# Order of VectorE and ScalarE in a turn of an attention kernel with two MLPs behind it

## The chip, the cores and the metric

One core of a Trainium2 chip. The metric is device time in microseconds of one execution, the median of the runs. TensorE multiplies, VectorE and ScalarE work element by element on SBUF and PSUM, GpSimd on SBUF alone, SyncE issues DMAs. Each engine executes its own instructions strictly in program order and waits for the others by semaphores.

## The reference

```
proj = x @ w_phi;  proj -= max(|proj|) over the features
phi(x) = [exp(proj), exp(-proj)]
kv = phi(k)^T v;  z = sum of phi(k) over the sequence
attn = (phi(q) kv) / (phi(q) z + 1e-6)
y = leaky(attn_rows @ w_in1, 0.01) @ w_out1
h = y @ w_in2;  out = (h * tanh(softplus(h))) @ w_out2
```

q, k, v are (4, 8, 576, 64) in fp32, w_phi is (64, 128), and the MLPs work on 2304 rows of 512 with 2048 hidden features. The weights of the MLPs arrive as 64-bit floats; the kernel turns them into fp32 itself.

## The kernel before

**Pairs and turns.** The 32 heads are worked on as 16 pairs. `attention(n)` (L513), called for n = 0 to 16, is one turn of a software pipeline over five pairs at once: t = n+2 has its q and k transposed, p = n+1 is projected, w = n gets its exponentials and its kv product, o = n-1 its numerator and denominator, x = n-2 is transposed into X, the input of the first MLP. Products of fp32 are made of three matmuls of split operands (`three`, L83, lines 84 to 86).

**What a turn does, in program order.** Loads for pair n+3 and values for t are issued on SyncE. `conv0.begin` is VectorE's part of the weight conversion: clamp of the high words to `c` (L135), a shift of the low words inside the stage (L137), and the mask and or to `e` (L138). `q_proj` (L389) makes four matmul groups; ScalarE copies each out of PSUM into `qd` (L401), and behind each second copy GpSimd computes the absolute maximum over the partitions, `qm` (L406, two per turn). `x_left` (L468) scales the left-over columns of x on ScalarE into `xleft`. `conv0.scale` (L143) makes on ScalarE the high part `wh` of the last converted weight (L213) and scales the newest `c` (L150). `k_proj` (L367) makes two groups, three in odd turns; VectorE takes their maximum `mx` and subtracts it (`kd`, L363 and L364). `k_exp` takes both exponentials of w on ScalarE (`kp`, in even turns `lp` as well, L386). `x_t` (L475) transposes `xn` on TensorE into `xt`, ScalarE copies it to X (L481), a matmul with `fold` puts the left-over columns into the last 64 columns of the PSUM tile `outs`, and a small ScalarE copy takes them to X (L484). `transposes` (L328) turns q and k of t, `split` on ScalarE and VectorE makes the high and low parts, and `q_left` adds two small casts (L359). `nd` (L434) writes numerator and denominator into `outs`, of which there is one: it must wait until every reader of the last contents is done, the small copy L484 among them. `normalise` (L454) reads them on VectorE (`den`, a reciprocal, `xn`). `q_guard` (L408) subtracts `qm` from `qd`, with both operands in SBUF. `conv0.join` puts sign and scaled value together on VectorE (L157) and makes the low part `wl` of the last weight (L214), or sends the converted weight to DRAM. Then come the exponentials of q, both halves of `kv` (L412) and a ScalarE copy of it (L432).

**Buffers that couple the engines.** The PSUM ring "a" has four banks. The q and k projections and the transposes of t take them in program order, so the transposes of k wait until the first k group has been read (L364), and k_proj until the q copies (L401) are done. `outs`, `kvp` and `xt` exist once. The stage has two buffers: the load of the next but one unit waits for the last reader of its buffer, and SyncE's later DMAs stand behind it in the queue.

**Conversion.** `conv0` has 15 units, one per turn from turn 1 on. The first ten are split into `wh` and `wl` one turn after their join, the last five are stored to DRAM.

**Around it.** Behind turns 8 to 11 `window(0, ...)` splits a quarter of the first block of X (ScalarE, then VectorE). Turns 15 and 16 end with `moe(0)` and `moe(1)`, the first hidden products of the first MLP: TensorE, then ScalarE, VectorE, ScalarE, VectorE (`leaky`). Behind turn 16 the last pair gets its `x_left` and `x_t`, and the loop of `moe` takes over.

Of the kernel before, what the change touches and what calls it, by code (L numbers as in the profile page):

```python
# [10 lines left out]
F32 = mybir.dt.float32  # L11
F32R = mybir.dt.float32r
AF = mybir.ActivationFunctionType
ALU = mybir.AluOpType
# [9 lines left out]
def attention_two_mlps_kernel(  # L24
# [12 lines left out]
    nc = tc.nc  # L37
    B, H, S, D = q.shape
    NT, DM = out.shape
    DFF = w1_in.shape[1]  # L40
    F = w_phi.shape[1]
    P = 128
    KD = DM // P
    M = DFF // P
    MAIN = 512
# [5 lines left out]
    CONV0 = 1  # L51
    HEAD = 2
    PAIRS = B * NP
# [6 lines left out]
    I32 = mybir.dt.int32  # L60
# [3 lines left out]
    gp = tc.alloc_tile_pool(name="gp", bufs=2)  # L64
# [3 lines left out]
    dr = tc.alloc_tile_pool(name="dr", bufs=1, space=bass.MemoryType.DRAM)  # L68
    ap = tc.alloc_tile_pool(name="ap", bufs=2, reuse_waits="tile")

    X = xp.tile([P, KD, NT], F32, name="X")
# [7 lines left out]
    def split(hi, lo, src):  # L79
        nc.scalar.activation(out=hi, in_=src, func=AF.Copy)  # L80
        nc.vector.tensor_tensor(out=lo, in0=src, in1=hi.bitcast(F32), op=ALU.subtract)
# [11 lines left out]
    class Conv:  # L93
# [4 lines left out]

        def __init__(self, which, units):
            self.which, self.units, self.at, self.loaded = which, units, 0, 0  # L100
            self.stage, self.open, self.half, self.rest = {}, None, None, None

        def load(self, ahead):

# [19 lines left out]
        def begin(self):  # L124

            self.load(1)
            if self.at == len(self.units):
                return
            u, kind = self.units[self.at]
            self.at += 1  # L130
            c = gp.tile([P, DM], F32, tag="c", name="c")
            e = gp.tile([P, DM], I32, tag="w1", name="e", bufs=1)
            stg = self.stage.pop(u)
            hw, lw = stg[:, :, 1], stg[:, :, 0]
            nc.vector.tensor_scalar(out=c, in0=hw.bitcast(F32), scalar1=F64_TOP, scalar2=-F64_TOP,  # L135
                                    op0=ALU.min, op1=ALU.max)
            nc.vector.tensor_scalar(out=lw, in0=lw, scalar1=29, scalar2=None, op0=ALU.logical_shift_right)  # L137
            nc.vector.scalar_tensor_tensor(out=e, in0=hw, scalar=-(1 << 31), in1=lw,  # L138
                                           op0=ALU.bitwise_and, op1=ALU.bitwise_or)
            self.load(1)  # L140
            self.open = (u, kind, c, e)

        def scale(self):  # L143

            if self.half is not None:
                u, c = self.half
                self.half, self.rest = None, split_w(self.which, u // 2, u % 2, c)
            if self.open is not None:
                c = self.open[2]
                nc.scalar.activation(out=c, in_=c, func=AF.Copy, scale=2.0 ** -112)  # L150

        def join(self):

            if self.open is not None:
                u, kind, c, e = self.open
                self.open = None
                nc.vector.scalar_tensor_tensor(out=c.bitcast(I32), in0=c.bitcast(I32), scalar=3, in1=e,  # L157
                                               op0=ALU.logical_shift_left, op1=ALU.bitwise_or)
                if kind == "store":
                    scr[self.which, u] = dr.tile([P, DM], F32, name=f"scr{self.which}_{u}")  # L160
                    nc.sync.dma_start(out=scr[self.which, u], in_=c)
                else:
                    self.half = (u, c)
            if self.rest is not None:
                self.rest()
                self.rest = None

        def step(self, *between):
            between = list(between) + [lambda: None] * 2
# [37 lines left out]
    def split_w(which, m, x, src):  # L207

        if x == 0:
            pool = wp0 if m < EARLY else wp  # L210
            W[which, m] = [pool.tile([P, 2, KD, P], F32R, tag=f"{t}{m}", name=f"w{t}{m}") for t in "hl"]
        hi, lo = (t[:, x].rearrange("p k f -> p (k f)") for t in W[which, m])
        nc.scalar.activation(out=hi, in_=src, func=AF.Copy)  # L213
        return lambda: nc.vector.tensor_tensor(out=lo, in0=src, in1=hi.bitcast(F32), op=ALU.subtract)  # L214
# [34 lines left out]
    with tc.manual_schedule():  # L249
# [105 lines left out]
        def q_left(i):  # L355
            s, l = st[i], lf[i // 2]
            c = P + (i % 2) * LEFT
            for x in "hl":
                nc.vector.tensor_copy(out=s["q" + x][:, HM:HM + LEFT], in_=l[x][:, c:c + LEFT].bitcast(F32))  # L359
# [69 lines left out]
        def kv_copy(i):  # L429
            s = st[i]  # L430
            s["kv"] = ap.tile([P, 4, D + 1], F32, tag="kv", name="kv", bufs=1)
            nc.scalar.activation(out=s["kv"], in_=s["kvp"][:, 0:4 * (D + 1)].rearrange("p (c n) -> p c n", n=D + 1), func=AF.Copy)  # L432
# [21 lines left out]
        def normalise(i):  # L454
            s = st[i]
            N = D + 1
            t = s["nd"]
            den = s["den"] = ap.tile([P, 2, 5], F32, tag="den", name="den")
            nc.vector.tensor_scalar(out=den, in0=t[:, :, D:5 * N:N], scalar1=1e-6, scalar2=None, op0=ALU.add)
            nc.vector.reciprocal(out=den, in_=den)  # L460
            s["xn"] = ap.tile([P, NM, 2, D], F32, tag="xn", name="xn")
            nc.vector.tensor_tensor(
                out=s["xn"].rearrange("p (c u) h d -> p c (u h) d", c=2),
                in0=t[:, :, 0:4 * N].rearrange("p c (m n) -> p c m n", n=N)[:, :, :, 0:D],
                in1=den[:, :, 0:4].unsqueeze(3).to_broadcast([P, 2, 4, D]), op=ALU.mult)
            s["xl"] = xleft[i % 2]

        def x_left(i):  # L468

            s = st[i]  # L470
            for h, r in enumerate(HALVES):
                nc.scalar.activation(out=s["xl"][r, h], in_=s["nd"][r, 1, 4 * (D + 1):4 * (D + 1) + D], func=AF.Copy,  # L472
                                     scale=s["den"][r, 1, 4:5])

        def x_t(i):  # L475
            s = st[i]
            b, p = divmod(i, NP)
            t = pa.tile([P, 512], F32, tag="xt", name="xt")
            for j in range(NM):
                nc.tensor.transpose(out=t[:, j * P:(j + 1) * P], in_=s["xn"][:, j].rearrange("p h d -> p (h d)"), identity=ident)  # L480
            nc.scalar.activation(out=X[:, p, b * MAIN:(b + 1) * MAIN], in_=t, func=AF.Copy)  # L481
            o = s["nd"][:, 1, MAIN - LEFT:MAIN]
            nc.tensor.matmul(out=o, lhsT=s["xl"].rearrange("p h d -> p (h d)"), rhs=fold, start=True, stop=True)
            nc.scalar.activation(out=X[:, p, C0 + b * LEFT:C0 + (b + 1) * LEFT], in_=o, func=AF.Copy)  # L484
            st[i] = None

        def k_exp(i, a):
            sg = 1 - 2 * a
            if i % 2 == 0:
                lf[i // 2].setdefault("lp", []).append(exp(lf[i // 2]["kd"], "lp", sg))  # L490
            st[i].setdefault("kp", []).append(exp(st[i]["kd"], "kp", sg))
# [21 lines left out]
        def attention(n):  # L513

            x, o, w, p, t = (i if 0 <= i < PAIRS else None for i in range(n - 2, n + 3))
            if n + 3 < PAIRS:
                load(n + 3)
            if t is not None and t > 1:  # L520
                values(t)
            if n >= CONV0:
                conv0.begin()
            if p is not None:
                for c in range(4):
                    q_proj(p, c)
            if x is not None:
                x_left(x)
            if n >= CONV0:
                conv0.scale()  # L530
            if p is not None:
                for c in range(2):
                    k_proj(p, c)
                if p % 2 == 0:
                    k_proj_left(p)
            if w is not None:
                for a in range(2):
                    k_exp(w, a)
            if x is not None:
                x_t(x)  # L540
            if t is not None:
                transposes(t)
                q_left(t)
            if o is not None:
                nd(o)
                normalise(o)
            if p is not None:
                q_guard(p)
            if n >= CONV0:
                conv0.join()  # L550
            if w is not None:
                st[w]["qp"] = [exp(st[w]["qd"], "qp", sg) for sg in (1, -1)]
                for a in range(2):
                    kv(w, a)
                kv_copy(w)
            if p is None:
                moe(n - PAIRS + 1)

# [212 lines left out]
        for n in range(PAIRS + 1):  # L771
            attention(n)
            if 0 <= n - PAIRS // 2 < KD:
                window(0, (n - PAIRS // 2,))
        x_left(PAIRS - 1)
        x_t(PAIRS - 1)
        ap.release()
        pa.release()
        rings["b"] = tc.alloc_tile_pool(name="pb", bufs=4, space=PSUM)
# [43 lines left out]
```

## Time and profile before

| | us |
|---|---|
| median of 3 runs (1012.76 to 1013.44) | 1013.23 |
| the profiled execution | 1010.47 |
| its span | 1008.6 |
| TensorE busy (PE) | 965.0 |
| VectorE busy (DVE) | 729.6 |
| ScalarE busy (ACT) | 510.6 |
| GpSimd busy (POOL) | 73.5 |
| stage loads: 64 of 512 KB, issue to landing | 3.7 and 3.6 |

Mean granted TensorE clock: 0.984 of full speed. The profile is one execution; the busy time of an engine counts from an instruction's start to its end, and neighbours may overlap by about 0.1 us, so that the sum of an engine can come close to a stretch that is full. A releaser is the event that the profile takes to have ended an engine's idle time; PEld is TensorE's weight load, which runs beside its matmuls. A wait on "issue" has no releaser that the profile shows.

### The profile page before, as it was taken

What the parts mean: (1) busy time and instruction counts of PE and PEld (TensorE: products, weight loads), DVE (VectorE), ACT (ScalarE), POOL (GpSimd) and SP (SyncE); (2) the same over time, 40 slices, a digit from 0 to 9 for tenths busy, and PEclk for the clock granted to TensorE, in tenths of its full rate; (3) what the DMA queues carried; (4) which work ended last, traced back from release to release, by engine and by line L of the source; (5) the groups of instructions that cost most, each with busy time, mean ns of one, the idle gap of its engine ahead of it and who ended that gap; (6) DMA issues with size and microseconds to landing.
All of it is one profiled execution on the core that took longest, in us unless ns stands there. A gap on an engine that the chain in (4) does not pass through costs nothing.

```text
span 1008.6 us, 16736 instructions
## 1 busy us (share of the span) xinstructions
PE 965.0 (96%) x6704; PEld 827.9 (82%) x6704; DVE 729.6 (72%) x1271; ACT 510.6 (51%) x886; POOL 73.5 (7%) x36
## 2 busy tenths in 40 slices
PE   8888878789999999999999999999999999999998
PEld 7788778668888889988888888888888988888886
DVE  7998998528984666666434457978877888878976
ACT  5887777635553333343234445545544555445543
POOL 3533333100000000000000000000000000000000
PEclk9999998889999999999999999999999999999999
DMA  6544423114431444444301330000100100001001
GB/s 199 142 134 119 113 79 111 36 64 139 153 105 53 143 148 133 142 144 147 115 0 45 121 96 11 1 1 1 42 1 1 43 1 22 0 1 42 1 1 42
DMA packets 68205, 72.97 MB, mean 72 GB/s; under 512 B 27168, under 2 KB 52640, under 8 KB 68128
## 3 DMA queue, kind: packets, MB, share of 16 engines
q1 hardware_dynamic: 67392, 71.52, 23.0%
q8 instruction: 52, 0.85, 0.3%
q10 hardware_dynamic: 736, 0.39, 0.1%
q14 instruction: 25, 0.20, 0.1%
HBM read 57.48 MB, written 14.42 MB: 71 GB/s over the span
## 4 chain that ended last, share of the span: by engine, by line
PE 91%; ACT 6%; DVE 1%; issue 1%; DMA 0%; ACTq 0%; DVEq 0%
PE a L84 14%; PE a L85 14%; PE a L86 14%; PE b L84 13%; PE b L86 13%; PE b L85 13%; PE outs L446 4%; PE kvp L423 2%; ACT kp L386 2%; ACT X L481 1%; PE a L339 1%; ACT xleft L472 1%; ACT c L150 1%; PE kvp L426 1%; ACT wh L213 0%
## 5 line engine op out<-in xcount | busy, mean ns | idle before, releaser
L84 PE MATMUL a<-wh,wh 128*128 128x512 f32 (+1 forms) x640 | 236.6, 370 | 0.0
L86 PE MATMUL a<-wh,wl 128*128 128x512 f32 (+1 forms) x640 | 236.3, 369 | 0.0
L85 PE MATMUL a<-wl,wh 128*128 128x512 f32 (+1 forms) x640 | 236.1, 369 | 0.0
L84 PEld LDWEIGHTS a<-wh,wh 128*128 128x128 f32 x640 | 121.0, 189 | 20.6 <-issue 0.2
L85 PEld LDWEIGHTS a<-wl,wh 128*128 128x128 f32 x640 | 121.1, 189 | 20.2
L86 PEld LDWEIGHTS a<-wh,wl 128*128 128x128 f32 x640 | 121.0, 189 | 20.2
L654 DVE TENSOR_TENSOR gl<-g,gh 128x512 fp32r<-128x512 f32 x72 | 49.9, 693 | 110.3 <-ACT gh L651 110.3
L84 PE MATMUL b<-gh,wh 128*128 128x512 f32 (+1 forms) x320 | 118.0, 369 | 0.0
L85 PE MATMUL b<-gl,wh 128*128 128x512 f32 (+1 forms) x320 | 117.9, 368 | 0.0
L86 PE MATMUL b<-gh,wl 128*128 128x512 f32 (+1 forms) x320 | 117.8, 368 | 0.0
L86 PE MATMUL b<-wh,gl 128*128 128x512 f32 x288 | 112.2, 390 | 0.0
L85 PE MATMUL b<-wl,gh 128*128 128x512 f32 x288 | 112.2, 390 | 0.0
L84 PE MATMUL b<-wh,gh 128*128 128x512 f32 x288 | 112.2, 390 | 0.0
L651 ACT ACTIVATE gh<-g 128x512 fp32r<-128x512 f32 x72 | 45.5, 632 | 116.1 <-PE b L86 110.9
L650 DVE TENSOR_TENSOR g<-g,a 128x512 f32<-128x512 f32 x72 | 49.4, 686 | 44.6 <-ACT g L647 41.8
L406 POOL PARTITION_ALL_REDUCE qm<-qd x32 | 73.3, 2338 | 113.5 <-ACT qd L401 105.2
L676 ACT ACTIVATE gh<-u 128x512 fp32r<-128x512 f32 x72 | 45.5, 632 | 70.3 <-PE b L85 63.5
L703 ACT ACTIVATE r<-e,two 128x512 f32<-128x512 f32 x72 | 51.7, 718 | 36.6 <-DVE e L688 36.6
L84 PEld LDWEIGHTS b<-gh,wh 128*128 128x128 f32 x320 | 60.5, 189 | 10.0
L85 PEld LDWEIGHTS b<-gl,wh 128*128 128x128 f32 x320 | 60.5, 189 | 10.0
L86 PEld LDWEIGHTS b<-gh,wl 128*128 128x128 f32 x320 | 60.4, 189 | 10.1
L672 ACT ACTIVATE e<-a 128x512 f32<-128x512 f32 x72 | 43.0, 597 | 47.8 <-PE a L86 26.3
(116 smaller groups left out, 1665.2 us busy)
## 6 DMA issues: line engine op xcount, KB each, us to landing
stage<-in_moe_w_in_dram SPq DMA_DIRECT2D x32, 512.0 KB, 3.7
stage<-in_moe_w_out_dram SPq DMA_DIRECT2D x32, 512.0 KB, 3.6
scr<-c SPq DMA_DIRECT2D x37, 256.0 KB, 2.0
wstage<-scr SPq DMA_DIRECT2D x32, 256.0 KB, 3.7
qn<-in_q_dram SPq DMA_DIRECT2D x16, 256.0 KB, 3.7
vmain<-in_v_dram SPq DMA_DIRECT2D x32, 128.0 KB, 2.9
kn<-in_k_dram SPq DMA_DIRECT2D x15, 256.0 KB, 3.3
out_dram<-X SPq DMA_DIRECT2D x15, 256.0 KB, 2.1
```

What stands on the lines that cost most here:

```text
L84: nc.tensor.matmul(out=o, lhsT=wh_, rhs=xh, start=start, stop=False)
L85: nc.tensor.matmul(out=o, lhsT=wh_, rhs=xl, start=False, stop=False)
L86: nc.tensor.matmul(out=o, lhsT=wl_, rhs=xh, start=False, stop=stop)
L386: nc.scalar.activation(out=e, in_=src, func=AF.Exp, scale=float(sg))
L406: nc.gpsimd.partition_all_reduce(qm, qd, P, bass_isa.ReduceOp.absmax)
L446: nc.tensor.matmul(out=g[r, u // 2, u % 2, h], lhsT=s["qp"][a][:, h, q0 + r.start:q0 + r.stop], rhs=s["kv"][:, 2 * h + a], start=(a == 0), ...
L650: nc.vector.tensor_tensor(out=g, in0=g, in1=h, op=ALU.max)
L651: nc.scalar.activation(out=hi, in_=g, func=AF.Copy)
L654: nc.vector.tensor_tensor(out=lo, in0=g, in1=hi.bitcast(F32), op=ALU.subtract)
L672: nc.scalar.activation(out=e0, in_=h0, func=AF.Exp)
L676: nc.scalar.activation(out=hi2, in_=u2, func=AF.Copy)
L703: nc.scalar.activation(out=r0, in_=e0, func=AF.Ln, bias=two)
```

## The change

Within a turn the calls of VectorE's and ScalarE's operations are put into another order; `Conv.scale` is divided in two, and the mask moves from `Conv.begin` to `Conv.join`.

- `Conv.begin` keeps the clamp and the shift. The mask to `e` and the next stage load move to `Conv.join`, in front of its last operation.
- A new `Conv.split`, right behind `begin`, makes `wh` and `wl` of the last weight.
- `normalise(x)` runs right behind the q projections, a turn later than before, and `x_left(x)` behind it. In turns 15 and 16, which project nothing, both run for o at the end of the turn, in front of `moe`.
- `k_exp(w, 0)` stays in front of `x_t`. `k_exp(w, 1)`, the large copy to X and the scaling of `c` come behind the transposes of t and in front of `nd`.
- `x_t` returns the large copy, to be called later.

```diff
--- before.py
+++ after.py
@@ -98,7 +98,7 @@
 
         def __init__(self, which, units):
             self.which, self.units, self.at, self.loaded = which, units, 0, 0
-            self.stage, self.open, self.half, self.rest = {}, None, None, None
+            self.stage, self.open, self.half = {}, None, None
 
         def load(self, ahead):
 
@@ -129,41 +129,43 @@
             u, kind = self.units[self.at]
             self.at += 1
             c = gp.tile([P, DM], F32, tag="c", name="c")
-            e = gp.tile([P, DM], I32, tag="w1", name="e", bufs=1)
             stg = self.stage.pop(u)
             hw, lw = stg[:, :, 1], stg[:, :, 0]
             nc.vector.tensor_scalar(out=c, in0=hw.bitcast(F32), scalar1=F64_TOP, scalar2=-F64_TOP,
                                     op0=ALU.min, op1=ALU.max)
             nc.vector.tensor_scalar(out=lw, in0=lw, scalar1=29, scalar2=None, op0=ALU.logical_shift_right)
+            self.open = (u, kind, c, hw, lw)
+
+        def split(self):
+
+            if self.half is not None:
+                u, c = self.half
+                self.half = None
+                split_w(self.which, u // 2, u % 2, c)()
+
+        def scale(self):
+
+            if self.open is not None:
+                c = self.open[2]
+                nc.scalar.activation(out=c, in_=c, func=AF.Copy, scale=2.0 ** -112)
+
+        def join(self):
+
+            if self.open is None:
+                return
+            u, kind, c, hw, lw = self.open
+            self.open = None
+            e = gp.tile([P, DM], I32, tag="w1", name="e", bufs=1)
             nc.vector.scalar_tensor_tensor(out=e, in0=hw, scalar=-(1 << 31), in1=lw,
                                            op0=ALU.bitwise_and, op1=ALU.bitwise_or)
             self.load(1)
-            self.open = (u, kind, c, e)
-
-        def scale(self):
-
-            if self.half is not None:
-                u, c = self.half
-                self.half, self.rest = None, split_w(self.which, u // 2, u % 2, c)
-            if self.open is not None:
-                c = self.open[2]
-                nc.scalar.activation(out=c, in_=c, func=AF.Copy, scale=2.0 ** -112)
-
-        def join(self):
-
-            if self.open is not None:
-                u, kind, c, e = self.open
-                self.open = None
-                nc.vector.scalar_tensor_tensor(out=c.bitcast(I32), in0=c.bitcast(I32), scalar=3, in1=e,
-                                               op0=ALU.logical_shift_left, op1=ALU.bitwise_or)
-                if kind == "store":
-                    scr[self.which, u] = dr.tile([P, DM], F32, name=f"scr{self.which}_{u}")
-                    nc.sync.dma_start(out=scr[self.which, u], in_=c)
-                else:
-                    self.half = (u, c)
-            if self.rest is not None:
-                self.rest()
-                self.rest = None
+            nc.vector.scalar_tensor_tensor(out=c.bitcast(I32), in0=c.bitcast(I32), scalar=3, in1=e,
+                                           op0=ALU.logical_shift_left, op1=ALU.bitwise_or)
+            if kind == "store":
+                scr[self.which, u] = dr.tile([P, DM], F32, name=f"scr{self.which}_{u}")
+                nc.sync.dma_start(out=scr[self.which, u], in_=c)
+            else:
+                self.half = (u, c)
 
         def step(self, *between):
             between = list(between) + [lambda: None] * 2
@@ -478,11 +480,11 @@
             t = pa.tile([P, 512], F32, tag="xt", name="xt")
             for j in range(NM):
                 nc.tensor.transpose(out=t[:, j * P:(j + 1) * P], in_=s["xn"][:, j].rearrange("p h d -> p (h d)"), identity=ident)
-            nc.scalar.activation(out=X[:, p, b * MAIN:(b + 1) * MAIN], in_=t, func=AF.Copy)
             o = s["nd"][:, 1, MAIN - LEFT:MAIN]
             nc.tensor.matmul(out=o, lhsT=s["xl"].rearrange("p h d -> p (h d)"), rhs=fold, start=True, stop=True)
             nc.scalar.activation(out=X[:, p, C0 + b * LEFT:C0 + (b + 1) * LEFT], in_=o, func=AF.Copy)
             st[i] = None
+            return lambda: nc.scalar.activation(out=X[:, p, b * MAIN:(b + 1) * MAIN], in_=t, func=AF.Copy)
 
         def k_exp(i, a):
             sg = 1 - 2 * a
@@ -515,44 +517,49 @@
 
 
             x, o, w, p, t = (i if 0 <= i < PAIRS else None for i in range(n - 2, n + 3))
+            x_copy = lambda: None
             if n + 3 < PAIRS:
                 load(n + 3)
             if t is not None and t > 1:
                 values(t)
             if n >= CONV0:
                 conv0.begin()
+                conv0.split()
             if p is not None:
                 for c in range(4):
                     q_proj(p, c)
-            if x is not None:
+            if x is not None and n < PAIRS:
+                normalise(x)
                 x_left(x)
-            if n >= CONV0:
-                conv0.scale()
             if p is not None:
                 for c in range(2):
                     k_proj(p, c)
                 if p % 2 == 0:
                     k_proj_left(p)
             if w is not None:
-                for a in range(2):
-                    k_exp(w, a)
+                k_exp(w, 0)
             if x is not None:
-                x_t(x)
+                x_copy = x_t(x)
             if t is not None:
                 transposes(t)
                 q_left(t)
+            if w is not None:
+                k_exp(w, 1)
+            x_copy()
+            conv0.scale()
             if o is not None:
                 nd(o)
-                normalise(o)
             if p is not None:
                 q_guard(p)
-            if n >= CONV0:
-                conv0.join()
+            conv0.join()
             if w is not None:
                 st[w]["qp"] = [exp(st[w]["qd"], "qp", sg) for sg in (1, -1)]
                 for a in range(2):
                     kv(w, a)
                 kv_copy(w)
+            if p is None:
+                normalise(o)
+                x_left(o)
             if p is None:
                 moe(n - PAIRS + 1)
 
@@ -772,8 +779,7 @@
             attention(n)
             if 0 <= n - PAIRS // 2 < KD:
                 window(0, (n - PAIRS // 2,))
-        x_left(PAIRS - 1)
-        x_t(PAIRS - 1)
+        x_t(PAIRS - 1)()
         ap.release()
         pa.release()
         rings["b"] = tc.alloc_tile_pool(name="pb", bufs=4, space=PSUM)
```

## Rows read from the trace of the kernel before

**Rows 1.** Busy time by stages: stretch, length, then busy us (instructions) per engine, PEclk, DMA, GB/s

```profile
31.93:114.78 82.85, 70.22 (x1292) 65.88 (x1292) 74.12 (x129) 68.72 (x131) 31.73 (x14) 0.98 0.45 123
114.78:158.85 44.07, 35.26 (x555) 33.28 (x555) 39.11 (x61) 30.35 (x57) 14.10 (x6) 0.85 0.30 84
158.85:180.78 21.93, 19.29 (x369) 18.36 (x369) 19.64 (x37) 18.78 (x36) 9.39 (x4) 1.00 0.43 125
180.78:193.71 12.93, 10.04 (x178) 9.73 (x174) 6.56 (x13) 8.41 (x17) 4.71 (x2) 0.87 0.06 22
193.71:204.56 10.85, 7.02 (x155) 6.37 (x151) 4.38 (x9) 6.35 (x11) 0.00 (x0) 0.84 0.07 26
204.56:220.73 16.17, 11.54 (x109) 9.62 (x110) 3.84 (x7) 5.04 (x12) 0.00 (x0) 0.89 0.30 98
220.73:290.00 69.27, 69.27 (x300) 57.16 (x299) 59.61 (x110) 35.84 (x63) 0.00 (x0) 0.98 0.44 134
```

**Rows 2.** Chain of waits in turn 5: start, length, what

```profile
68.80 0.44 ACT qd L401
...
69.77 0.64 ACT wh L213
70.41 0.52 ACT c L150
70.93 1.89 ACT kp L386 x2
...
72.85 0.60 ACT X L481
...
73.61 2.09 PE outs L446 x64
```

**Rows 3.** Waits from 31 to 221 us: who for whom, us in total, times, longest

```profile
PE outs L446 <- ACT X L484: 15.2, 12, 3.3
...
PE a L339 <- issue: 10.0, 4, 3.0
```

**Rows 4.** Timeline of turn 5: start, us, what, idle before and releaser

```profile
68.36 0.43 DVE L135 TENSOR_SCALAR c<-stage 128x512 f32<-128x512 f32 x1
68.53 4.56 POOL L406 PARTITION_ALL_REDUCE qm<-qd  x2 [7.33 <-ACT qd L401]
68.70 1.52 DVE L137 TENSOR_SCALAR stage<-stage 128x512 int32<-128x512 int32 x1
70.39 0.60 PE L480 MATMUL xt<-ident,xn 128*128 128x128 f32 x4
70.87 0.68 DVE L363 TENSOR_REDUCE mx<-a 128x4 f32<-128x512 f32 x1
```

**Rows 5.** Timeline of turn 13, VectorE

```profile
171.20 0.42 DVE L137 TENSOR_SCALAR stage<-stage 128x512 int32<-128x512 int32 x1
```

**Rows 6.** Timeline of turn 9, VectorE

```profile
116.64 1.52 DVE L135 TENSOR_SCALAR c<-stage 128x512 f32<-128x512 f32 x1
```

**Rows 7.** Groups of instructions from 31 to 195 us: busy us, mean ns, idle before

```profile
L462 DVE TENSOR_TENSOR xn<-outs,den 128x512 f32<-128x512 f32 x14 | 9.7, 692 | 0.5
L214 DVE TENSOR_TENSOR wl<-c,wh 128x512 fp32r<-128x512 f32 x10 | 6.8, 684 | 0.0
L460 DVE RECIPROCAL den<-den 128x10 f32<-128x10 f32 x13 | 2.8, 216 | 0.4
```

**Rows 8.** Busy time of turns 4 and 5, columns as in rows 1

```profile
55.08:66.97 11.89, 9.77 (x186) 9.14 (x185) 10.51 (x19) 10.20 (x20) 4.56 (x2) 1.00 0.49 127
66.97:78.24 11.27, 9.89 (x187) 9.27 (x186) 10.84 (x20) 9.31 (x17) 4.56 (x2) 1.00 0.41 121
```

**Rows 9.** Timeline of turns 14 to 16, TensorE

```profile
187.69 3.65 PE L446 MATMUL outs<-kv,qp 128*64 128x65 f32 x64 [2.88 <-ACT X L484]
...
198.74 3.28 PE L446 MATMUL outs<-kv,qp 128*64 128x65 f32 x64 [3.35 <-ACT X L484]
...
220.30 0.43 PE L483 MATMUL outs<-fold,xleft 128*128 128x64 f32 x2 [2.17 <-ACT xleft L472]
```

More of the change, by code (lines that the diff above doesn't have):

```diff
@@ L137, in begin @@
             nc.vector.tensor_scalar(out=lw, in0=lw, scalar1=29, scalar2=None, op0=ALU.logical_shift_right)
-            nc.vector.scalar_tensor_tensor(out=e, in0=hw, scalar=-(1 << 31), in1=lw,
-                                           op0=ALU.bitwise_and, op1=ALU.bitwise_or)
-            self.load(1)
-            self.open = (u, kind, c, e)
-        def scale(self):
+            self.open = (u, kind, c, hw, lw)
+        def split(self):
             if self.half is not None:
                 u, c = self.half
-                self.half, self.rest = None, split_w(self.which, u // 2, u % 2, c)
+                self.half = None
+                split_w(self.which, u // 2, u % 2, c)()
+        def scale(self):
             if self.open is not None:
@@ L152, in join @@
         def join(self):
-            if self.open is not None:
-                u, kind, c, e = self.open
-                self.open = None
-                nc.vector.scalar_tensor_tensor(out=c.bitcast(I32), in0=c.bitcast(I32), scalar=3, in1=e,
-                                               op0=ALU.logical_shift_left, op1=ALU.bitwise_or)
-                if kind == "store":
-                    scr[self.which, u] = dr.tile([P, DM], F32, name=f"scr{self.which}_{u}")
-                    nc.sync.dma_start(out=scr[self.which, u], in_=c)
-                else:
-                    self.half = (u, c)
-            if self.rest is not None:
-                self.rest()
-                self.rest = None
+            if self.open is None:
[3 more added lines that the diff above has]
+            e = gp.tile([P, DM], I32, tag="w1", name="e", bufs=1)
+            nc.vector.scalar_tensor_tensor(out=e, in0=hw, scalar=-(1 << 31), in1=lw,
+                                           op0=ALU.bitwise_and, op1=ALU.bitwise_or)
+            self.load(1)
+            nc.vector.scalar_tensor_tensor(out=c.bitcast(I32), in0=c.bitcast(I32), scalar=3, in1=e,
[5 more added lines that the diff above has]
+                self.half = (u, c)
         def step(self, *between):
```

## The prediction

> **What bounds the kernel now.** I call one call of `attention(n)` turn n, and count a turn from TensorE's first projection matmul (q_proj) to the next turn's. I read the busy time by stages first: from 220.73 us on TensorE is busy for all of 69.27 us of 69.27, and it stays the bound in the two MLPs behind that, so the change can win only before that point, and what it wins there moves everything behind it forward, microsecond for microsecond [rows 1]. Before it, turns 2 to 8 take 82.85 us with TensorE busy for 70.22, turns 9 to 11 take 44.07 with 35.26, and from 180.78 to 220.73 some 40 us hold 28.6 us of matmuls [rows 1]. That is the room: 12.6, 8.8, 2.6 and 11.4 us of idle TensorE, and the matmuls that ran at the lower clock level on top (granted clock 0.98, 0.85, 1.00 and 0.84 to 0.89).
>
> Then I ask what ends TensorE's idle time. In one ordinary turn the chain of waits runs through ScalarE: the weight's high part `wh`, the scaling `c`, both exponentials `kp`, the copy `X` out of the transposes, the small copy of the left-over columns, and right behind that the first matmul of `nd` [rows 2]. The list of waits agrees: `nd` waited 15.2 us for that small copy (L484), in 12 turns, and the transposes of k waited 10.0 us in 4 turns with no releaser named [rows 3]. `nd` needs only the small copy; `wh`, `c`, the second `kp` and the large copy stand in front of it by program order alone.
>
> The second cost is VectorE's. In turn 5 the shift of the low words (L137) took 1.52 us beside GpSimd's maxima, which ran from 68.53 to 73.09 [rows 4], and 0.42 us in turn 13, where it ended before they began [rows 5]. The maximum `mx`, which reads PSUM, took 0.68 us beside them [rows 4]. In turn 9 the clamp (L135) met them instead, 1.52 us [rows 6] against 0.43 [rows 4]. So one collision costs 1.1 us (1.52 - 0.42; 1.52 - 0.43).
>
> **The change, part by part.** No instruction is added or removed: the counts stay, places move.
>
> ScalarE. Out of the stretch in front of `nd` go `wh` (0.64), `c` (0.52), half of the `kp` pair (0.95, and a small `lp` in even turns) and `X` (0.60): 2.7 us of the chain [rows 2]. `wh` now stands ahead of the four q copies, so these and the maxima start some 0.55 us later; what is behind it on ScalarE are the copies that free the q banks, for which k_proj waits. TensorE's first 3.4 us of a turn (66.97 to the transposes `xt` at 70.39 [rows 4]) cover that: q_proj alone lasts until 68.80 [rows 2], and the first q bank is free again before. If ScalarE comes late from the turn before, k_proj stands for an estimated 0.2 to 0.6 us.
>
> VectorE. `normalise` moves from behind `nd` to the next turn's beginning, in front of the k maxima, and `xt` now waits for it in its own turn. From the join on, VectorE has clamp 0.43, shift 0.42, `wl` 0.68, two tiny operations of about 0.2 and `xn` 0.69 [rows 4, 5, 7]: 2.6 us, inside the 3.4. The two-input masks (`e`) go to the turn's end, behind the subtraction that waits for the maxima anyway, so they can't meet them. `wl` starts behind clamp and shift, 0.85 us after the join; the maxima start behind `wh` and two q copies, 0.64 + 2 x 0.44 [rows 2], 1.5 us after it. So in a turn that splits, `wl` is under way first. So the shift's 1.1 us goes.
>
> SyncE's queue. The stage load moves with `e` to the turn's end, more than half a turn later, and the next turn's loads of k and q stand behind it. The stage is read a whole turn later (about 10 us), k and q later still; I cost this at nothing. Were it not hidden, each turn would wait for the landing, 3.7 us by the list of DMA issues in the table above.
>
> What is late next? In turn 5 TensorE's busy time is 9.89 us, ScalarE's 9.31 and VectorE's 10.84 less 1.1, 9.74; in turn 4 9.77, 10.20 and 10.51 less 1.1, 9.4 [rows 8]. So a turn can't fall below about 9.8, and I take 10.0 for the seams: the join frees `wh`, `wh` the q copies, the kv copy ends late in even turns.
>
> The sum, against the profiled execution (1010.47 us):
> (A) Turns 2 to 8: 82.85 - 7 x 10.0 = 12.85.
> (B) Turns 9 to 11 carry one more split of X each (ScalarE 0.6, VectorE 0.69), and VectorE's half of it waits for ScalarE's at the turn's beginning. That pushes clamp, shift and `wl` to where the maxima start, so I leave one collision: 9.74 + 0.69 + 1.1 = 11.5, or 10.5 where VectorE wins the race; I take 11.4, the nearer to the rows of turn 9. I also leave one `nd` at the lower clock level (3.65 against 2.09 us, 1.5 [rows 2, 9]). 44.07 - 34.2 - 1.5 = 8.4.
> (C) Turns 12 and 13: no `wh` holds the maxima back, and 12 has a split of X: 11.0 and 9.9 against 21.93: 1.0.
> (D) Turn 14: `nd` waits 2.88 us and then takes 3.65 [rows 9]. Without the 2.1 us and more of ScalarE in front of it and without the idle stretch: 2.1 + 1.6 = 3.7.
> (E) Turn 15: `nd` waits 3.35 [rows 9]. `c`, one `kp` and `X` go (2.1), `xt` waits a little for `xn`; the clock I leave low: 2.0.
> (F) Behind it the scaling of the left-over columns (`xleft`) moves ahead of the first MLP's activation on ScalarE. TensorE stood 2.17 us for it at 220.30 [rows 9], and about as long once before; of the first I count half, 1.1, as the small copy still stands behind that activation: 3.3.
> Sum 31.25, so 979.2. The median of the runs shown, 1013.23, lies 2.76 above the profiled execution: 982.
>
> **Where the bounds are unknown.** The reciprocal, SBUF to SBUF and 0.216 us long [rows 7], never ran beside the maxima before; after the change it does. Below: nothing. Above: the shift's 1.1 us, in each turn. I take nothing, because it is ten elements long and stands between operations on PSUM. The Trainium skill (SBUF — State Buffer, "Who interferes with whom") lets copy, cast and tensor_scalar take the port pair that VectorE shares with GpSimd, and frees an operation with one SBUF input outside the two-port modes; reciprocal is not on its list. By that rule the sum stays 982; by the shift's row it would be 991. No row here shows which.
>
> **Rivals.**
> 1. The reciprocal (or `wl`) meets the maxima in every turn. For it: the seam above is only tenths wide. Against: `mx` at 0.68 beside them. VectorE then needs 9.74 + 1.1, a turn 10.9: A falls to 6.5, B to 6.9, C to 0, the tail (D to F, 9.0) stays: 22.4, 991.
> 2. Turns 9 to 11 don't gain: two collisions and an idle stretch long enough for the lower clock level stay (granted clock 0.85 now). B is 0: 22.9, 990. With rival 1 on top: 998.
> 3. Slower. VectorE comes to the turn's beginning late, the maxima are already running, and the clamp waits as in turn 9 [rows 6], the shift behind it. Now `xn` and all k maxima stand behind them, `xt` on TensorE behind `xn`, and an idle stretch of 3 us brings `nd` at the lower clock level in every turn. A turn then takes what turns 9 to 11 take, 44.07 / 3 = 14.7: 7 x 14.7 - 82.85 = 20 lost, B and C 0, the tail won: 11 slower, 1024. It decides from the point where the clamp starts later than the maxima, and costs more than the tail gives from 0.9 us a turn on (9.0 / 10). Against: in split turns the maxima start behind `wh`, and `wh` behind the join, so VectorE's lateness moves both.
> 4. The stall moves only: `nd` starts earlier, but kv's second half waits for the second `kp`, the kv copy for ScalarE, and the turn stays as long. Then only the tail is won, 9.0: 1004. Against: TensorE has the 2.09 us of `nd` [rows 2] and the first half of kv in front of that.
>
> **How the numbers follow.** Forecast 0.62; rival 1 0.12; rival 2 0.12; rival 3 0.07; rival 4 0.07. The forecast's own range is 974 (all clock losses gone and no collision: 8 us more) to 988. Taking in rivals 1 and 2 and their sum: 972 to 1000. A measurement of this kernel tells about 0.2%, 2 us, from no change. Slower 0.07 (rival 3), the same 0.03 (between rivals 3 and 4), faster 0.90.
>
> **What would show it.** Right: the shift at 0.42 us in turns 3 to 8 and nothing but PSUM readers and the reciprocal beside the maxima; turns 2 to 8 near 10 us at a granted clock of 1.00; the wait of `nd` for L484 gone from the list; no wait for `xleft` behind turn 15. Wrong: `xt` waiting for `xn` over 0.5 us a turn, a reciprocal of over 1 us, k_proj standing for q copies by more than a few tenths, a `wl` of over 1 us, or TensorE waiting at a turn's end for q's split.

## The result, and the profile after

The changed kernel takes 981.75 us (median of 4 runs, 980.69 to 982.93) against 1013.34 for the kernel before: ratio 0.969 (95% interval 0.967 to 0.971), 31.6 us faster. The two profiled executions lie closer together: 982.12 against 1010.47 us, spans 980.0 and 1008.6, so a sum over the traces has 28.6 us to explain, and the other 3 us are that the profiled execution of before was faster than its kernel's median.

The busy time by stages of the changed kernel, columns as in [rows 1]: turns 2 to 8, 9 to 11, 12 and 13, 14, 15, the stretch to the third hidden product, and behind it.

```profile
33.73:105.35 71.62, 70.00 (x1292) 64.55 (x1292) 66.64 (x131) 65.64 (x131) 29.83 (x14) 1.00 0.50 140
105.35:142.74 37.39, 31.23 (x556) 27.81 (x555) 33.29 (x59) 29.80 (x58) 12.94 (x6) 1.00 0.43 117
142.74:164.10 21.36, 19.71 (x370) 18.48 (x370) 19.66 (x38) 18.33 (x37) 8.94 (x4) 1.00 0.45 129
164.10:173.32 9.22, 8.48 (x175) 8.10 (x174) 8.09 (x16) 8.63 (x17) 4.26 (x2) 1.00 0.29 88
173.32:182.71 9.39, 7.23 (x151) 6.75 (x151) 3.42 (x9) 6.45 (x10) 0.00 (x0) 0.82 0.37 128
182.71:193.65 10.94, 9.37 (x110) 8.05 (x110) 2.45 (x5) 3.81 (x10) 0.00 (x0) 1.00 0.20 62
193.65:290.00 96.35, 96.35 (x427) 79.75 (x427) 75.92 (x136) 48.40 (x85) 0.00 (x0) 1.00 0.34 104
```

Against [rows 1] the stages are 11.2, 6.7, 0.6, 3.7, 1.5 and 5.2 us shorter. Turns 2 to 8 hold 1.6 us of idle TensorE where there were 12.6, and the granted clock is 1.00 in every stage but turn 15. Turn 2 begins 1.8 us later than before (33.73 against 31.93), and the rest behind 193.65, 786.35 us, is 1.5 shorter. The sum is the 28.6.

Rows from the timeline of turn 5 of the changed kernel: VectorE, ScalarE, GpSimd and TensorE, answering to [rows 4].

```profile
64.74 0.42 DVE L134 TENSOR_SCALAR c<-stage 128x512 f32<-128x512 f32 x1
65.08 0.43 DVE L136 TENSOR_SCALAR stage<-stage 128x512 int32<-128x512 int32 x1
65.55 0.66 ACT L215 ACTIVATE wh<-c 128x512 fp32r<-128x512 f32 x1
66.25 0.69 DVE L216 TENSOR_TENSOR wl<-c,wh 128x512 fp32r<-128x512 f32 x1 [0.75 <-ACT wh L215]
66.91 4.26 POOL L408 PARTITION_ALL_REDUCE qm<-qd  x2 [6.23 <-ACT qd L403]
67.05 0.22 DVE L462 RECIPROCAL den<-den 128x10 f32<-128x10 f32 x1
67.30 0.69 DVE L464 TENSOR_TENSOR xn<-outs,den 128x512 f32<-128x512 f32 x1
68.03 0.63 ACT L474 ACTIVATE xleft<-outs,den 64x64 f32<-64x64 f32 x2 [0.61 <-DVE xn L464]
...
69.77 0.22 ACT L485 ACTIVATE X<-outs 128x64 f32<-128x64 f32 x1
70.06 2.09 PE L448 MATMUL outs<-kv,qp 128*64 128x65 f32 x64
70.84 1.07 ACT L388 ACTIVATE kp<-kd 128x1024 f32<-128x1024 f32 x1
71.79 0.61 ACT L487 ACTIVATE X<-xt 128x512 f32<-128x512 f32 x1
```

The shift takes 0.43 us where it took 1.52, `wl` is done as the maxima begin, the reciprocal stands beside them at its old 0.22, and `nd` no longer stands behind the second `kp` and the large copy. `nd` still waits for the small copy in turns 14 to 16, 3.2 us in all, where it was 15.2 in twelve turns [rows 3]. New in the list of waits from 31 to 195 us:

```profile
ACT xleft L474 <- DVE xn L464: 18.0, 13, 3.3
...
PE xt L482 <- DVE xn L464: 7.0, 5, 1.6
...
PE outs L448 <- ACT X L485: 3.2, 3, 1.6
PE a L84 <- ACT qd L403: 2.9, 7, 0.8
```

In turns 9 to 11 one collision stayed, with `wl`, and one in turn 12, with the shift (1.52 us). Here is turn 9, VectorE, GpSimd and the places where TensorE stands; the first row is the low part of the split of X.

```profile
107.10 0.69 DVE L81 TENSOR_TENSOR wl<-X,wh 128x512 fp32r<-128x512 f32 x1 [1.43 <-ACT wh L80]
107.71 0.42 DVE L134 TENSOR_SCALAR c<-stage 128x512 f32<-128x512 f32 x1
107.97 0.39 PE L84 MATMUL a<-wbh,kth 128*128 128x256 f32 x1 [0.82 <-ACT qd L403]
108.05 0.42 DVE L136 TENSOR_SCALAR stage<-stage 128x512 int32<-128x512 int32 x1
108.28 4.31 POOL L408 PARTITION_ALL_REDUCE qm<-qd  x2 [6.74 <-ACT qd L403]
108.38 1.78 DVE L216 TENSOR_TENSOR wl<-c,wh 128x512 fp32r<-128x512 f32 x1
...
111.28 0.66 PE L482 MATMUL xt<-ident,xn 128*128 128x128 f32 x4 [1.27 <-DVE xn L464]
```

VectorE stands 1.43 us for ScalarE's half of the split, `wl` then meets the maxima (1.78 us), and behind it TensorE stands 1.27 us for `xn`. It had stood 0.82 us for the q copies before, which come behind ScalarE's half of the split. The same turn of the kernel before held more than the clamp's collision [rows 6]: shift and mask met the maxima too, and TensorE stood 2.90 us for a bank.

```profile
118.08 1.12 DVE L137 TENSOR_SCALAR stage<-stage 128x512 int32<-128x512 int32 x1
...
119.24 1.64 DVE L138 SCALAR_TENSOR_TENSOR e<-stage 128x512 int32<-128x512 int32 x1
...
122.31 0.63 PE L339 MATMUL a<-ident,kn 128*128 128x128 f32 x4 [2.90 <-issue]
```

### The profile page after: what moved, and what is told of

It is laid out like the page before. It is cut to its first block, busy times and chain, and to the rows that moved or that the text cites. A ratio compares the mean times of both kernels' runs of the same rounds, so it can differ in the third digit from the quotient of the medians.

```text
span 980.0 us, 16741 instructions
## 1 busy us (share of the span) xinstructions
PE 957.1 (98%) x6704; PEld 818.4 (84%) x6704; DVE 715.9 (73%) x1271; ACT 507.2 (52%) x886; POOL 69.0 (7%) x36
## 4 chain that ended last, share of the span: by engine, by line
PE 83%; DVE 7%; ACT 7%; issue 1%; DMA 0%; POOL 0%; POOLq 0%; ACTq 0%; DVEq 0%
PE a L84 14%; PE a L85 14%; PE a L86 14%; PE b L86 13%; PE b L85 13%; PE b L84 13%; ACT kp L388 2%; ACT qp L388 1%; DVE wl L216 1%; DVE xn L464 1%; DVE mx L365 1%; PE outs L448 1%; DVE qd L412 1%; DVE kd L366 1%; ACT xleft L474 1%
## 5 line engine op out<-in xcount | busy, mean ns | idle before, releaser
L408 POOL PARTITION_ALL_REDUCE qm<-qd x32 | 68.8, 2197 | 100.7 <-ACT qd L403 94.0
```

The costliest lines, as they stand in the source:

```text
L408: nc.gpsimd.partition_all_reduce(qm, qd, P, bass_isa.ReduceOp.absmax)
```

## The experiments

Twelve kernels ran, each beside the kernel before on the same chip. The median of before differed from group to group (1011.97 to 1013.34 us), so kernels are compared by their ratios.

**ScalarE's order alone.**

```diff
 # the kernel before, with
+conv0.split()              # wh, right behind begin; wl stays behind the join
-for a in range(2): k_exp(w, a)
+k_exp(w, 0)
 ... x_t without the large copy, transposes, q_left ...
+k_exp(w, 1); x_copy(); conv0.scale()
 ... nd, normalise, q_guard, join with mask early ...
```

> ScalarE's order of the changed kernel, VectorE's and the ends of turns 15 and 16 as before. My theory: two limits stood one behind the other, ScalarE's queue in front of nd and VectorE's collisions with the maxima, and lifting one alone uncovers the other. VectorE then bounds: turns 2 to 8 about 11.1 us (10.5 and 10.8 busy and a seam), 5 us won; turns 9 to 11 stay near 13.3 on VectorE, 3 won; turns 14 and 15, where VectorE is idle, 5 won: about 1000, with the shift (L137) still 1.5 us beside the maxima. Rival A, ScalarE's order is the whole change: 983 to 987. Rival B, the collisions are: 1009 or more.

Measured 987.81 us, ratio 0.975 (0.973 to 0.977). My theory fell, by 12 us; this is rival A, nearly. Four fifths of the gain come with VectorE's order untouched.

**VectorE's order alone.**

```diff
 # the changed kernel, with
 normalise(x); x_left(x)
+conv0.scale()
 ... k_proj ...
-k_exp(w, 0)
+for a in range(2): k_exp(w, a)
 ... the large copy to X back in front of the small one, x_left of the last two pairs behind moe ...
 # wh stays right behind begin, since wl is made from it
```

> VectorE's order of the changed kernel, ScalarE's as before but for the high part of the weight, which has to stand ahead of its low part. My theory: no collisions in ordinary turns, but nd waits for ScalarE's small copy as before, now also behind xn: turns 2 to 8 11.2 to 11.8, 0 to 4 us won; turns 9 to 11 lose the 3 us stand for the bank and most of the lower clock, 4 to 6 won; nothing at the end: 1003 to 1009. Rival A (ScalarE alone): 1010 to 1013. Rival B (collisions alone): 983 to 987.

Measured 1013.63, ratio 1.000 (0.999 to 1.002): nothing. Its clamp, shift and mask are free of collisions (0.42, 0.50 and 0.69 us on average) but for one shift in turn 12; `wl` meets the maxima in turns 9 to 11 only. And yet `nd` waits, from 31 to 200 us:

```profile
PE outs L448 <- ACT X L486: 27.2, 13, 2.9
```

That is more than before (15.2 in [rows 3]): the time that VectorE gave back went into a longer wait for ScalarE. In the same list ScalarE itself waits 13.7 us in 11 turns with `xleft` for `xn`, in front of what opens `nd`. Turns 2 to 8 took 85.70 us, against 82.85.

**The end alone.**

```diff
 # the kernel before, with
-if x is not None: x_left(x)
+if x is not None and n < PAIRS: x_left(x)
 if p is None:
+    x_left(o)
     moe(n - PAIRS + 1)
-x_left(PAIRS - 1)
```

> Before, with only the scaling of the left-over columns of the last two pairs moved in front of the first MLP's activation. My theory: 2.2 us of wait at the last fold and half of the one before it go, and with the idle stretch the matmuls at the lower clock level behind it (2 us): 3 to 5 us, 1008 to 1010. Rival: the copies behind it on ScalarE take its place, 0 to 1 us, 1012 to 1013.

Measured 1007.66, ratio 0.995 (0.994 to 0.997): 5.6 us between the medians, 4.8 by the ratio, as expected. The last two folds no longer wait. The `nd` between them now waits 2.06 us for the small copy, where it was 0.31: a part of the rival.

**The mask back early.**

```diff
 # the changed kernel: the mask to e and the next stage load from join back into begin
```

> The changed kernel with the mask e back behind the shift, at the beginning of the turn. My theory: wl then starts 0.65 us later and meets the first maxima in every turn that splits (1.78 us as in turns 9 to 11 of the changed kernel instead of 0.69), VectorE is on the path, and turns 2 to 11 cost about 1 us more each: 989 to 993. Rival: VectorE has room for 1 us a turn, 981 to 984.

Measured 983.32, ratio 0.971 (0.970 to 0.973): the rival, so far as the total goes. By stages both happened. Turns 2 to 8 took 70.88 us, less than the changed kernel's 71.62; turns 9 to 11 took 39.83 against 37.39. In turns 2 to 11 clamp and shift kept their place in front of the maxima and `wl` stayed at 0.69 us; in turns 9 to 11 it was the mask that met the maxima (1.66 us), and in turn 12 the shift, as in the changed kernel.

**ScalarE's order and the end, VectorE's as before.** The edits of "ScalarE's order alone" and "The end alone" together; the kernel differs from the changed one in VectorE's order alone.

> ScalarE's order and the ends of turns 15 and 16 of the changed kernel, VectorE's order as before; it differs from the changed kernel in VectorE's order alone. Theory after the first runs: the gain is ScalarE's order (0.975) times the end (0.995), and VectorE's order is worth next to nothing: 981 to 985, with one or two turns that wait over 3 us for a bank. Rival: VectorE's order is worth the 6 us that ScalarE's order alone lacked, and the end's 5.6 us overlaps with what ScalarE's order has: 986 to 988.

Measured 980.71, ratio 0.969 (0.967 to 0.971), where the changed kernel has 0.969. ScalarE's order times the end, 0.975 x 0.995 = 0.970, is the whole change; its VectorE part brings nothing on balance. The busy time of turns 2 to 8, 9 to 11, 12 and 13 of this kernel shows what is inside that nothing:

```profile
32.78:107.47 74.69, 69.88 (x1292) 64.40 (x1292) 72.30 (x129) 66.78 (x131) 29.83 (x14) 1.00 0.47 135
107.47:140.83 33.36, 30.12 (x556) 27.68 (x555) 32.78 (x60) 29.89 (x58) 13.12 (x6) 1.00 0.42 113
140.83:165.16 24.33, 20.91 (x370) 20.02 (x370) 22.00 (x38) 18.80 (x37) 9.48 (x4) 0.93 0.39 113
```

VectorE's new order won 3.1 us in turns 2 to 8 (74.69 to 71.62) and 3.0 in turns 12 and 13, and lost 4.0 in turns 9 to 11 (33.36 to 37.39) and 2.4 in turns 14 and 15, where `xt` now stands behind `xn` and one `nd` ran at the lower clock level (3.66 us against 2.09).

**Two of ScalarE's four moves.**

```diff
 # the kernel before, with k_exp(w, 1) and the large copy behind the transposes;
 # wh and the scaling of c stay between x_left and k_proj
```

> Before, with only the second pair of exponentials and the large copy to X moved behind the transposes of t; the high part of the weight and its scaling stay in front of nd. Theory: these two are 1.55 us of the 2.7 in front of nd, more than TensorE's idle 1.4 us of an odd turn: most of ScalarE's part, 988 to 994. Rival: every microsecond in front of nd counts alike, 1.55 of 2.7: 25 x 0.57 = 14, 999.

Measured 1002.17, ratio 0.990 (0.988 to 0.991): 10 us, nearer to the rival, and for a reason that neither had. Turns 2 to 8 gain nothing (83.00 us against 82.85); most of the gain is in turns 14 and 15 (17.26 against 23.78). Its list of waits, 31 to 215 us:

```profile
PE a L339 <- issue: 19.1, 7, 3.4
```

Its turn 4, VectorE, GpSimd and TensorE:

```profile
55.52 4.63 POOL L406 PARTITION_ALL_REDUCE qm<-qd  x2 [6.11 <-ACT qd L401]
55.73 1.40 DVE L135 TENSOR_SCALAR c<-stage 128x512 f32<-128x512 f32 x1
...
57.06 1.12 DVE L137 TENSOR_SCALAR stage<-stage 128x512 int32<-128x512 int32 x1
...
58.21 1.64 DVE L138 SCALAR_TENSOR_TENSOR e<-stage 128x512 int32<-128x512 int32 x1
...
60.56 0.69 DVE L364 TENSOR_TENSOR kd<-a,mx 128x512 f32<-128x512 f32 x1
...
61.35 0.63 PE L339 MATMUL a<-ident,kn 128*128 128x128 f32 x4 [2.89 <-issue]
...
61.91 3.56 PE L446 MATMUL outs<-kv,qp 128*64 128x65 f32 x64
```

With `nd`'s gate opened earlier, TensorE arrives at the transposes of k before VectorE has read the first k group out of its bank (`kd` ends at 61.25, the transposes begin at 61.35). Here the collisions are the price: clamp, shift and mask all meet the maxima (2.6 us together over 0.43, 0.42 and 0.69), TensorE stands 2.89 us, and `nd` runs at the lower clock level (3.56 us). So a collision that costs nothing behind a later gate can take a turn's whole gain once that gate is gone. With ScalarE's full order (the first experiment), turn 4 looks like this:

```profile
55.57 0.43 DVE L135 TENSOR_SCALAR c<-stage 128x512 f32<-128x512 f32 x1
55.91 0.42 DVE L137 TENSOR_SCALAR stage<-stage 128x512 int32<-128x512 int32 x1
56.29 4.26 POOL L409 PARTITION_ALL_REDUCE qm<-qd  x2 [6.68 <-ACT qd L404]
56.37 1.76 DVE L138 SCALAR_TENSOR_TENSOR e<-stage 128x512 int32<-128x512 int32 x1
```

One collision instead of three. From the join to the maxima 1.1 us pass in the first kernel and 2.0 in the second (joins at 54.41 and 54.26): the high part of the weight, put ahead of the q copies, holds the maxima back until clamp and shift are through. Against the kernel with two moves, ScalarE's full order frees VectorE of two of three collisions, and VectorE's order need not do it; against the kernel before, whose turn 4 has one collision too (the shift, 1.53 us), the number is the same.

**The maxima later without `wh`.**

```diff
 # that kernel (two moves), q_proj:
-if {2 * h, 2 * h + 1} <= half:
-    partition_all_reduce(qm[h], qd[h])
+if len(half) == 4:
+    for h in range(2): partition_all_reduce(qm[h], qd[h])
```

> The kernel with the second exponentials and the large copy moved (expected above at 988 to 994, measured 1002), with both maxima of a turn issued behind the fourth q copy and not behind the second and the fourth; ScalarE's and VectorE's orders stay. Theory: there TensorE stands 19 us in seven turns for a bank that VectorE reads late, because clamp, shift and mask meet the maxima; a high part of the weight ahead of the q copies cures that by bringing the maxima 0.5 us later. Maxima 0.8 us later without it then let clamp and shift go first and win most of those stands and the lower clock behind them: 988 to 995. Rival: the stands come from ScalarE, the kernel stays at 1000 to 1004.

Measured 1001.52, ratio 0.989 (0.988 to 0.991), as without the edit. It tells nothing on the theory: the maxima began 0.80 us behind the first q copy (56.34 and 55.54), as they had (55.52 and 54.71). They wait for their own two copies, and issuing them later in the program did not move them. That `wh` works through the maxima's start is therefore read from two traces that also differ in the place of `c`, and not shown by itself.

**The left-over columns in front of `xn`.**

```diff
 # the changed kernel, normalise:
 nc.vector.reciprocal(out=den, in_=den)
+x_left(i)
 nc.vector.tensor_tensor(out=xn, ...)
```

> The changed kernel with the scaling of the left-over columns issued between the reciprocal and xn. Theory: ScalarE then starts it behind the reciprocal and not behind xn, 0.6 us earlier in 13 turns; the even turns, in which ScalarE is on the path, get about 0.5 us shorter: 977 to 980. Rival: ScalarE has that time to wait elsewhere (for the transposes of q), no change: 981 to 983.

Measured 986.60, ratio 0.975 (0.973 to 0.977): 6 us slower than the changed kernel, a miss of theory and rival. The wait turned round, from 31 to 200 us:

```profile
DVE xn L466 <- ACT xleft L475: 15.7, 16, 2.9
...
PE xt L483 <- DVE xn L466: 12.3, 10, 2.3
```

Both read the PSUM tile `outs` and the small `den`, and the one that is issued second waits for the first; which of the two tiles orders them the traces don't tell. Of the two orders the one with `xn` first is better, since TensorE waits for `xn`.

**The splits of X inside the turns.**

```diff
 # the changed kernel, attention:
 conv0.join()
+if 0 <= n - PAIRS // 2 < KD: window(0, (n - PAIRS // 2,))
 ... exponentials of q, kv ...
 # and no window behind attention(n)
```

> The changed kernel with the four splits of X issued ahead of the exponentials of q, inside turns 8 to 11 instead of behind them. Theory: VectorE no longer waits for ScalarE at the beginning of turns 9 to 12, clamp, shift and low part are done before the maxima begin, wl takes 0.69 us and not 1.78, and these four turns get 1.5 to 2 us shorter: 974 to 977. Rival: ScalarE's 0.5 us in front of the exponentials takes the place: 979 to 982.

Measured 973.89, ratio 0.962 (0.960 to 0.964): 7 us faster than the changed kernel, as the theory has it. `wl` takes 0.69 us in every turn. In the trace turns 9 to 11 are 5.2 us shorter (32.15 us) and turns 12 and 13 1.6 (19.80), together what the theory said of four turns. Another 1.6 is the `nd` of turn 15, at the upper clock level here; whether the edit brings that the traces don't show, for the stands in front of it are the same (last section).

**The same with VectorE's order as before.**

> ScalarE's order and the ends of the changed kernel, VectorE's order as before, and the splits of X inside the turns. Theory: VectorE's order is worth something only where three collisions come together, and these go with the splits' place, so that this kernel equals the changed one with the splits inside: 972 to 977. Rival: VectorE's order wins 0.3 us a turn in ordinary turns and one long stand in turn 12, 978 to 981.

Measured 980.20, ratio 0.968 (0.967 to 0.970): the rival. Once the splits are out of the way, VectorE's order is worth 0.6%. By the traces it wins 3.1 us in turns 2 to 8, 1.2 in turns 9 to 11 and 2.65 in turns 12 and 13, and loses 0.8 in turns 14 and 15.

**Turn 0 mended.** In turn 0 of the changed kernel TensorE waits for the second exponential, which had stood in front of the transposes before:

```profile
23.01 1.16 PE L425 MATMUL kvp<-vmain,kp 128*64 128x65 f32 x32 [0.79 <-ACT kp L388]
```

```diff
 # the kernel with the splits inside, attention:
 k_exp(w, 0)
+if n == 0: k_exp(w, 1)
 ... x_t, transposes ...
-if w is not None: k_exp(w, 1)
+if w is not None and n > 0: k_exp(w, 1)
```

> The changed kernel with the splits of X inside the turns (973.9 measured) and with both exponentials of turn 0 in front of the transposes, as before the change. Theory: turn 0 lost 0.8 us of TensorE waiting for the second exponential, and up to 1 us more at the lower clock: 972 to 973. Rival: nothing, 974.

Measured 972.45, ratio 0.961 (0.959 to 0.962), the fastest median of all: 39.5 us faster than before, and by the ratios 8 faster than the changed kernel. Its step over the kernel with the splits inside is within the two intervals; in the traces its turn 2 begins 2.3 us earlier (30.67 and 33.02). Its turns 2 to 8, 9 to 11, 12 and 13:

```profile
30.67:102.30 71.63, 70.02 (x1292) 64.57 (x1292) 66.67 (x131) 65.66 (x131) 29.83 (x14) 1.00 0.50 140
102.30:134.47 32.17, 30.11 (x556) 27.79 (x555) 29.96 (x59) 29.83 (x59) 12.99 (x6) 1.00 0.49 136
134.47:154.29 19.82, 19.72 (x370) 18.49 (x370) 18.48 (x38) 18.32 (x36) 8.66 (x4) 1.00 0.50 139
```

**And with the mask early.** The kernel before this one with the mask back in `begin`.

> The changed kernel with the splits inside, turn 0 mended, and the mask early in the turn. Theory: with the mask early ordinary turns took 10.13 us and not 10.23, and its losses lay in the turns with splits, which are now free of collisions: 970 to 973. Rival: the mask meets the maxima there still, 974 to 977.

Measured 973.01, ratio 0.961 (0.959 to 0.962): no difference from the one before it. With the other collisions gone, the mask may stand at either end.

## Why the prediction was right, and where it was not

The total came out as forecast, 981.75 against 982, in part by chance. Of the steps behind it, ScalarE's queue and the end held; VectorE's part did not.

- *The sum by stages.* Forecast for A to F 12.85, 8.4, 1.0, 3.7, 2.0, 3.3 us; the traces give 11.2, 6.7, 0.6, 3.7, 1.5, 5.2, then 1.5 us behind the end and a loss of 1.8 in front of turn 2. So the sum of 31.25 was 2.6 too large for the two traces: A, B and C came 3.7 short and E 0.5, 1.8 was lost in front of turn 2, and F and what is behind it gave 3.4 more. (For the two profiled executions it was 2.9 too large, 979.2 against 982.12.) It met the median because I set the profiled execution's distance to its median, 2.76 us, on top of the result, and the changed kernel's profiled execution has none. That part of the hit is chance.
- *ScalarE's queue in front of `nd`.* Right, and the largest part: 0.975 alone. What I did not see is that a part of the moves brings less than its share: two of the four, 1.55 of the 2.7 us, brought 10 of 25 us. What the other two bring alone was not run.
- *"So the shift's 1.1 us goes."* It went, but it was not worth what I let it be worth. VectorE's order alone gave 1.000, and taken out of the changed kernel it cost nothing (0.969). I had read VectorE's 9.74 us as a bound that only its new order could reach. With the order as before, and one collision in a turn, turns 2 to 8 still took 10.7 us a turn against 10.2.
- *A.* Mis-sized: 10.0 us a turn, seams and all, was too little. TensorE alone is busy for 70.00 us of these seven turns afterwards, 10.0 a turn and not the 9.8 read from turns 4 and 5, and the seams come on top: 10.23.
- *The reciprocal* beside the maxima took 0.22 us, as forecast. Rival 1 is out; the rule of the Trainium skill that I weighed (SBUF — State Buffer, "Who interferes with whom"), by which the sum stayed 982, agrees with this trace: 0.22 us at 67.05, beside maxima that began at 66.91.
- *Turns 9 to 11.* One collision stayed in each, as I took it (`wl` 1.78 us), and the lower clock level went from all three. What I mis-sized is the stand around it: 12.5 us a turn in place of 11.4 and a third of 1.5, with TensorE standing for the q copies and for `xn` (0.82 and 1.27 us in turn 9). I had also named only the clamp's collision in turn 9 of before, where shift and mask met the maxima too. Two of the signs of being wrong stood here: `wl` over 1 us, and `xt` waiting 1.3 to 1.6 us for `xn` in turns 9 to 12 and 15. Rival 2 named the place; there the changed kernel is slower than its own ScalarE half (33.36 us).
- *k_proj behind the q copies* stood 2.9 us in 7 turns, 0.4 a turn where I had estimated 0.2 to 0.6; the longest was 0.8.
- *SyncE's queue* cost nothing, as taken: the list of waits from 31 to 195 us has none for a DMA.
- *E.* A little too large, 1.5 against 2.0: `xt` waited 1.27 us for `xn` there, and the lower clock level stayed, as taken.
- *F.* Mis-sized from below: 5.2 us there and 1.5 behind it, since with the idle stretch the lower clock level went too. Alone it measured 5.6 us between the medians, 4.8 by the ratio.
- *Not foreseen:* the second exponential of turn 0 behind the transposes (0.79 us of wait), and `xleft` waiting for `xn`.
- *Rivals 3 and 4* (1024 and 1004 us) are out by the measured ratio of 0.969.

## What to carry to other kernels

Look at what stands between an engine's last operand and the one small instruction that opens the gate for the bound engine: what does not feed the gate can go behind it, and that pays until the next limit. A collision that can be seen, 1.1 us in every turn, was worth nothing here as long as another gate opened later; take the parts of a change out one at a time before you name one of them as its cause. Work that comes in few turns (the splits of X) can undo in these what a new order wins in all others; moving it by one place in the turn won 7 us, the most after ScalarE's order.

## What the runs showed of the hardware

- A VectorE operation on SBUF that runs beside the maxima can lose 0.7 to 1.1 us: clamp 1.40 to 1.52 us for 0.43, shift 1.10 to 1.53 for 0.42, mask 1.64 to 1.76 for 0.69, `wl` 1.78 for 0.69. Not each one does: in turn 5 of the kernel before the mask began 1.7 us behind their start, beside them, and took 0.69. Readers of PSUM (`mx` 0.68) and the ten-element reciprocal (0.22) lost nothing.
- The maxima can pay too. Two take 4.26 us in most turns of the changed kernel, where nothing meets them, and 4.56 [rows 4] or 4.63 where shift or clamp does, but 4.31 beside `wl` and 4.26 beside the mask (turn 4 of ScalarE's order alone, shown above).
- TensorE's lower clock level (granted clock 0.54 over the `nd` of 3.56 us, 1.00 over one of 2.09) often followed stands of about 2.9 us (`nd` at 3.56 us behind 2.89, 3.65 behind 2.88 [rows 9]), but not each time: the same turn 4 with the maxima issued later stood 2.90 us and kept the upper level (first two rows). Shorter stands, 1.27 and 0.90 us with the transposes between them, came before the lower level in turn 15 of the changed kernel (third row), and before the upper one in the kernel with the splits inside (last row). The changed kernel's turns 9 to 12, with 1.3 to 1.6 us for `xn`, kept the upper level. So no length of a stand that decides it can be read from these runs.

```profile
62.19 0.63 PE L339 MATMUL a<-ident,kn 128*128 128x128 f32 x4 [2.90 <-issue]
62.75 2.09 PE L447 MATMUL outs<-kv,qp 128*64 128x65 f32 x64
...
176.50 3.66 PE L448 MATMUL outs<-kv,qp 128*64 128x65 f32 x64 [0.90 <-ACT X L485]
...
168.99 2.09 PE L448 MATMUL outs<-kv,qp 128*64 128x65 f32 x64 [0.89 <-ACT X L485]
```
